# Cached GQA block on one core: x loaded in six pieces, five V loads made whole

## The chip, the core and the metric

The kernel runs on one core of a Trainium2 chip. The metric is the device time of one execution in microseconds (us). The core has a matmul engine (PE), a vector engine (DVE), a scalar engine (ACT), GpSimd (POOL) and a sync engine (SP); SP, and once ACT, issue the DMA transfers between device memory and the on-chip buffers. Sixteen DMA engines carry them.

## What is computed

One attention block of a decoder with a KV cache: 8 sequences of 4 new tokens, 32 query heads on 8 KV heads, 2048 cached positions, head size 128, all in bf16.

```python
B, Sq, D = 8, 4, 512
Hq, Hkv, Sk, Dh = 32, 8, 2048, 128
q = (x @ wq).reshape(B, Sq, Hq, Dh).transpose(0, 2, 1, 3)
k = jnp.repeat(k_cache, Hq // Hkv, axis=1)
v = jnp.repeat(v_cache, Hq // Hkv, axis=1)
scores = jnp.einsum("bhqd,bhkd->bhqk", q, k) * (Dh ** -0.5)
p = softmax(scores, axis=-1)
o = jnp.einsum("bhqk,bhkd->bhqd", p, v)
return o.transpose(0, 2, 1, 3).reshape(B, Sq, Hq * Dh) @ wo
```

x is 32 rows of 512 (32 KB). The K cache and the V cache have 33.6 MB each, wq and wo 4.2 MB each.

## The kernel before

The work is cut into eight units, u = 0 to 7. A unit is 16 pairs of a sequence and a KV head handled in two "members", 4 MB of K and 4 MB of V. Units 1 to 6 take one sequence each (`single(u)`); units 0 and 7 take half of the heads of the last two sequences. For a unit, DVE transposes K in 32 by 32 blocks (`turn`, L213), PE multiplies it with the queries (`scores`, L251), DVE takes the maxima (`top`), ACT the exponentials (`exps`, L291), DVE and the others bring the weights into place (`weights`, L305 and L315), and PE multiplies them with V (`values`, L331). `values` works on the unit before, so that two units overlap. Each matmul of `values` reads both members of V at one key position.

The order of the work on every engine is the program's order (`manual_schedule`); the framework adds the semaphores and the waits.

The big loads share a **ring** of four slots of 4 MB (`ring`, `NR = 4`). `loads` lists them in order: K0 (with x), wq, K1, V0, K2, V1, K3, V2, ... K7, V6, V7, wo. `issue(done)` takes the next of them as long as fewer than `done + 4` have been taken; a load into a slot waits until the slot's earlier content has landed and been read. `issue(0)` at the start issues K0, x, wq, K1 and V0; the call at the end of each unit's turn issues the next two.

`load_kv` can issue a load as one DMA (`whole`), as two halves of every row (`by_half`), or as one DMA for each member (`by_member`, 2 MB each). K0 goes by member, one on SP and one on ACT; V0 to V4 and K7 are in the list `split` and go by member on SP; V7 goes by half; wo goes in five pieces (L146). x is loaded on SP behind SP's half of K0 (L163), and is first used by four PE transposes (L416), whose result feeds the query projection with wq (L425). The projection's result is turned (L436) and copied into `q_bd` (L231), from where the scores of unit 0 take it.

At the end `project` (L403) multiplies the rows with wo; the last piece of wo is followed by a few matmuls, two copies out of PSUM (L482, L483) and the store of the result (L484).

Of the kernel before, what the change touches and what calls it, by code (L numbers as in the profile page):

```python
# [17 lines left out]
def kernel(  # L18
# [9 lines left out]
    nc = tc.nc  # L28
# [6 lines left out]
    T = B * Sq  # L35
# [6 lines left out]
    NU = B * Hkv // (G * NB)  # L42
# [31 lines left out]
    x_sb = const.tile([T, D], BF16, name="x_sb")  # L74
# [35 lines left out]
    def load_kv(kind, u, parts, engines=(nc.sync,)):  # L110

        slot = take((kind, u))
        cache = k_cache if kind == "k" else v_cache
        n = C * Dh
        if not single(u):
            rows = cache[NS1:, G * half_of(u) : G * half_of(u) + G].rearrange(
                "b g (s c) d -> (g s) b (c d)", c=C
            )
        elif kind == "v":
            rows = cache[u - 1].rearrange("(b g) (s c) d -> (g s) b (c d)", g=G, c=C)  # L120
        else:
            rows = cache[u - 1].rearrange("h (s c) d -> (h s) (c d)", c=NS * C)
        if kind == "k" and single(u):
            pairs = [(ring[:, slot, :, :].rearrange("p b n -> p (b n)"), rows)]
        elif parts is by_member:
            pairs = [(ring[:, slot, b, :], rows[:, b]) for b in range(NB)]
        else:
            pairs = [
                (ring[:, slot, :, int(h0 * n) : int(h1 * n)], rows[:, :, int(h0 * n) : int(h1 * n)])
                for h0, h1 in parts  # L130
            ]
        for i, (to, of) in enumerate(pairs):
            engines[i % len(engines)].dma_start(to, of)

    def load_wq():
        slot = take("wq")
        nc.sync.dma_start(
            ring[:, slot, :, :].rearrange("p b n -> p (b n)"), wq.rearrange("(p r) n -> p (r n)", r=R)
        )

    def load_wo():
        slot = take("wo")
        for gg, cuts in ((0, (0, RW)), (1, (0, 8, 13, 15, RW))):
            rows = wo[gg * G * 512 : (gg + 1) * G * 512, :].rearrange("(p r) j -> p (r j)", r=RW)
            for r0, r1 in zip(cuts, cuts[1:]):
                nc.sync.dma_start(ring[:, slot, gg, r0 * D : r1 * D], rows[:, r0 * D : r1 * D])  # L146
# [5 lines left out]
            loads.append(("k", u + 2))  # L152
    loads.append("wo")
    loads.reverse()
    split = [("v", 0), ("v", 1), ("v", 2), ("v", 3), ("v", 4), ("k", NU - 1)]

    def issue(done):

        while loads and n_loads[0] < done + NR:
            what = loads.pop()  # L160
            if what == "k0":
                load_kv("k", 0, by_member, (nc.sync, nc.scalar))
                nc.sync.dma_start(x_sb[:, :], x.flatten_outer_dims())  # L163
            elif what == "wq":
                load_wq()
            elif what == "wo":
                load_wo()
            elif what in split:
                load_kv(*what, by_member)
            else:  # L170
                load_kv(*what, by_half if what == ("v", NU - 1) else whole)

    issue(0)

    make_identity(nc, ident[:])
# [266 lines left out]
    for u in range(NU + 1):  # L442
# [19 lines left out]
        if u >= 1:  # L462
# [7 lines left out]
            if u == NU:  # L470
                joined(u - 1)
        issue(2 + 2 * u)

    o_last = psum_o.tile([128, DH], FP32, tag="o", name="o_last")
# [40 lines left out]
```

## Time and profile before

| | |
|---|---|
| Time, median of 3 runs | 184.73 us (184.65 to 189.89) |
| Profiled execution | 184.38 us, span from first to last instruction 182.5 us |
| Busy: PE, DVE, ACT, POOL | 136.6, 128.7, 70.3, 39.3 us |
| Read from device memory | 75.53 MB, 414 GB/s over the span |
| DMA transfers: K 10, V 14, wq 1, wo 5, x 1, result 1 | most of 2 or 4 MB |

The span counts from the first instruction to the last; the time of the execution includes 1.9 us around it. "Busy" of an engine is the time in which it had an instruction at work. The strip of the DMA line has 40 slices of 4.6 us; a 9 is 90% or more. For a DMA the profile gives the moment of issue on its queue (SPq, ACTq) and the time from issue until it has landed.

### The profile page before, as it was taken

The numbers are of one execution on the slowest core, as the hardware profiler recorded it, in microseconds if no ns is written. First come the engines' busy times: TensorE is split into PE (matmuls) and PEld (weight loads), VectorE is DVE, ScalarE is ACT, GpSimd is POOL, SyncE is SP. The second block draws the span as 40 slices with busy tenths as digits, with TensorE's granted clock in tenths as the row PEclk, the third lists the DMA queues.
The fourth block names the chain that finished last, engine by engine and source line by source line (L and its number), as shares of the span: only waits on it lengthen the run. The fifth ranks groups of instructions, "written<-read, shape, count | busy, mean of one in ns | idle before, by whom it ended". The sixth has DMA issues, their size and how long they took to land.

```text
span 182.5 us, 2386 instructions
## 1 busy us (share of the span) xinstructions
PE 136.6 (75%) x924; PEld 83.3 (46%) x924; DVE 128.7 (71%) x161; ACT 70.3 (39%) x91; POOL 39.3 (22%) x110
## 2 busy tenths in 40 slices
PE   0000076940999999998999898989399977899993
PEld 0000022310348635843783485358234852388971
DVE  6518025738994999599689957995399559967340
ACT  2000020019604940990395079109900792063010
POOL 8800006006200700430080035004400220023000
PEclk9999999995589999999999999999969999999999
DMA  6999999999999998999999999999999999999991
GB/s 226 431 485 395 424 460 406 424 445 449 452 384 427 456 461 382 420 460 452 391 417 453 460 402 418 431 478 424 391 435 424 435 427 435 415 426 438 427 385 42
DMA packets 4938, 75.70 MB, mean 415 GB/s; under 512 B 512, under 2 KB 704, under 8 KB 960
## 3 DMA queue, kind: packets, MB, share of 16 engines
q1 hardware_dynamic: 4784, 73.47, 94.3%
q10 hardware_dynamic: 144, 2.10, 2.8%
q8 instruction: 7, 0.11, 0.2%
q14 instruction: 3, 0.02, 0.0%
HBM read 75.53 MB, written 0.03 MB: 414 GB/s over the span
## 4 chain that ended last, share of the span: by engine, by line
DMA 42%; DVE 23%; PE 22%; issue 4%; ACT 3%; POOL 2%; SPq 1%; ACTq 0%; DVEq 0%; POOLq 0%
DMA ring<-in_wo_dram 16%; PE s_ps L251 16%; DMA ring<-in_k_cache_dram 15%; DVE kt L213 14%; DMA ring<-in_wq_dram 12%; DVE stat L264 4%; PE o_ps L331 4%; ACT p_sb L291 3%; PE psq L425 2%; DVE pt L305 2%; DVE stat L322 1%; POOL p_bd L315 1%; POOL q_bd L231 1%; PE s_ps L403 1%; DVE stat L272 0%
## 5 line engine op out<-in xcount | busy, mean ns | idle before, releaser
L251 PE MATMUL s_ps<-kt,q_bd 128*128 128x512 bf16 x256 | 69.5, 409 | 20.0 <-POOL q_bd L231 9.9
L213 DVE STREAM_TRANSPOSE kt<-ring 128x1024 f32<-128x1024 f32 x64 | 73.9, 1210 | 14.2 <-DMA ring<-in_k_cache_dram 11.4
L331 PE MATMUL o_ps<-ring,p_bd 128*128 128x256 bf16 x512 | 57.2, 273 | 0.0
L251 PEld LDWEIGHTS <-q_bd 128*128 128x128 bf16 x256 | 25.3, 102 | 63.0 <-issue 26.6
L331 PEld LDWEIGHTS <-p_bd 128*128 128x128 bf16 x512 | 49.8, 98 | 6.0 <-issue 0.2
L315 ACT COPY p_bd<-pt 32x1024 bf16<-32x1024 bf16 x44 | 45.8, 1041 | 1.5 <-DVE pt L305 1.1
L291 ACT ACTIVATE p_sb<-s_ps,stat 128x1024 bf16<-128x1024 f32 x16 | 17.7, 1110 | 72.2 <-DVE stat L272 72.2
L315 POOL COPY p_bd<-pt 32x1024 bf16<-32x1024 bf16 x16 | 17.0, 1065 | 105.9 <-DVE pt L305 93.2
L264 DVE TENSOR_REDUCE stat<-s_ps 128x1 f32<-128x1024 f32 x16 | 19.3, 1208 | 3.4 <-PE s_ps L251 3.4
L305 DVE STREAM_TRANSPOSE pt<-p_sb 128x512 f32<-128x512 f32 x16 | 11.4, 712 | 14.0 <-ACT p_sb L291 14.0
L231 POOL COPY q_bd<-qT 32x64 bf16<-32x64 bf16 x64 | 13.1, 231 | 20.7 <-DVE qT L436 19.0
L425 PE MATMUL psq<-ring,xT_sb 128*32 128x512 bf16 x32 | 3.6, 630 | 9.1 <-DMA ring<-in_wq_dram 9.1
L416 PE MATMUL xtp<-ident,x_sb 32*128 32x32 bf16 x4 | 0.3, 195 | 13.3 <-DMA x_sb<-in_x_dram 13.3
L436 DVE STREAM_TRANSPOSE qT<-q_sb 128x64 f32<-128x64 f32 x8 | 1.2, 214 | 8.8 <-ACT q_sb L432 8.8
L177 DVE MEMSET p_bd<- 128x2048 uint32 x3 | 5.3, 1765 | 2.0 <-PEq L499 1.2
L322 DVE TENSOR_SCALAR stat<-of_b,stat 128x2 f32<-128x2 f32 x8 | 6.3, 793 | 0.3
L416 PEld LDWEIGHTS <-x_sb 32*128 32x128 bf16 x4 | 0.2, 117 | 13.3 <-DMA x_sb<-in_x_dram 13.3
L425 PEld LDWEIGHTS <-xT_sb 128*32 128x32 bf16 x32 | 1.3, 140 | 10.5 <-issue 10.1
L432 ACT CAST q_sb<-psq 128x512 bf16<-128x512 f32 x2 | 1.2, 586 | 11.8 <-PE psq L425 11.8
L375 PEld LDWEIGHTS <-perm 128*128 128x128 bf16 x56 | 3.8, 97 | 2.0 <-issue 0.5
L419 ACT COPY xT_sb<-xtp 128x128 bf16<-128x128 bf16 x1 | 0.3, 266 | 11.2 <-PE xtp L416 11.2
L343 ACT ACTIVATE o_sb<-o_ps,stat 128x128 bf16<-128x128 f32 x8 | 2.9, 368 | 4.1 <-PE o_ps L331 3.9
(30 smaller groups left out, 46.4 us busy)
## 6 DMA issues: line engine op xcount, KB each, us to landing
ring<-in_k_cache_dram SPq DMA_DIRECT2D x6, 4096.0 KB, 22.7
ring<-in_v_cache_dram SPq DMA_DIRECT2D x12, 2048.0 KB, 23.6
ring<-in_v_cache_dram SPq DMA_DIRECT2D x2, 4096.0 KB, 29.6
ring<-in_k_cache_dram SPq DMA_DIRECT2D x3, 2048.0 KB, 27.2
ring<-in_wq_dram SPq DMA_DIRECT2D x1, 4096.0 KB, 21.0
ring<-in_k_cache_dram ACTq DMA_DIRECT2D x1, 2048.0 KB, 12.4
ring<-in_wo_dram SPq DMA_DIRECT2D x1, 2048.0 KB, 25.9
ring<-in_wo_dram SPq DMA_DIRECT2D x1, 1024.0 KB, 28.2
```

What stands on the lines that cost most here:

```text
L177: nc.vector.memset(t[:, :, :, :, :], 0.0)
L213: nc.vector.transpose(out=out, in_=in_)
L231: nc.gpsimd.tensor_copy(out=qb[k * 32 : (k + 1) * 32, m, :, g, b, :].rearrange("w (j e) q -> w j e q", e=2), in_=qT[of * 32 : (of + 1) * 3 ...
L251: nc.tensor.matmul(s_ps[t // 2][:, t % 2, :], lhsT=q_bd[u % 2][:, m, 2 * j + e, :, :, :].rearrange("w g b q -> w (g b q)"), rhs=rhs, start ...
L264: nc.vector.tensor_reduce(out=stats[u][0][:, h : h + 1], in_=s_ps[h][:, :, :].rearrange("q t n -> q (t n)"), axis=AX, op=ALU.max, negate=True,
L291: nc.scalar.activation(out=out, in_=in_, func=EXP, bias=stats[u][1][:, :], scale=scale, accum_out=stats[u][2][:, h : h + 1],)
L305: nc.vector.transpose(out=pt[:, :, :, :].rearrange("s c q e -> s (c q e)").bitcast(FP32), in_=ps[u, h][:, :, :, :].rearrange("q c s e -> q ...
L315: copy(out=pb[rows, :, g, :, :], in_=pt[rows, :, :, :])
L322: nc.vector.tensor_scalar_mul(stats[u][3][:, :], of_b[:, :], stats[u][4][:, :])
L331: nc.tensor.matmul(o_pss[u][:, :, :], lhsT=pbs[u, h][:, i // 2, :, :, i % 2].rearrange("s g q -> s (g q)"), rhs=v[:, :, key_of(u, h, i // ...
L375: nc.tensor.matmul(o_pms[r // 2][:, r % 2, gg, :], lhsT=perm[:, r, w : w + 128], rhs=o_sbs[u][:, b, :], start=(u == 0 and r % 2 == 0 and g ...
L425: nc.tensor.matmul(psq[g * T : (g + 1) * T, :], lhsT=xT_sb[:, r, :], rhs=w[:, (g * NB + gg) * rep * Dh : (g * NB + gg + 1) * rep * Dh], st ...
```

## The change

x is loaded by six DMAs of 16, 8, 4, 2, 1 and 1 rows instead of one of 32, at the same place, behind K0 and ahead of wq. V0 to V4 are no longer in `split`: each is one DMA of 4 MB instead of two of 2 MB. K7 stays split. The number of DMAs is the same as before, and no other line is changed.

```diff
-    split = [("v", 0), ("v", 1), ("v", 2), ("v", 3), ("v", 4), ("k", NU - 1)]
+    split = [("k", NU - 1)]
...
             if what == "k0":
                 load_kv("k", 0, by_member, (nc.sync, nc.scalar))
-                nc.sync.dma_start(x_sb[:, :], x.flatten_outer_dims())
+
+                cuts = (0, 16, 24, 28, 30, 31, T)
+                for t0, t1 in zip(cuts, cuts[1:]):
+                    nc.sync.dma_start(x_sb[t0:t1, :], x.flatten_outer_dims()[t0:t1])
```

## The prediction

> **What bounds the kernel now.** I read the page's strips and its chain first, then the DMA issues, then stretches of a microsecond at both ends, then SP's queue.
>
> ```profile
> DMA  6999999999999998999999999999999999999991
> GB/s 226 431 485 395 424 460 406 424 445 449 452 384 427 456 461 382 420 460 452 391 417 453 460 402 418 431 478 424 391 435 424 435 427 435 415 426 438 427 385 42
> ...
> HBM read 75.53 MB, written 0.03 MB: 414 GB/s over the span
> ...
> DMA 42%; DVE 23%; PE 22%; issue 4%; ACT 3%; POOL 2%; SPq 1%; ACTq 0%; DVEq 0%; POOLq 0%
> ```
>
> The DMA engines are full from the first slice to the last but one, while DVE (71%) and PE (75%) have room. The chain names DVE and PE for long stretches only because it goes back through SP's waits for a free ring slot; those waits end before the DMA queue is empty. At 35.01 us SP issues K2, and V0 is still in transfer until 2.68 + 36.7 = 39.4 us for the median of its two halves; at 53.43 it issues K3, with V1 in transfer until 62.4. The DMA engine never starves between 2 and 178 us, so whatever delays its stream moves the end by as much, and whatever else changes moves nothing.
>
> The start and the end of that stream, each row a stretch in us, then the busy time of the engines, the granted clock, the DMA share and GB/s:
>
> ```profile
> 0.00:1.00 1.00, 0.00 (x0) 0.00 (x0) 0.00 (x0) 0.00 (x0) 0.42 (x5) 1.00 0.00 0
> 1.00:2.00 1.00, 0.00 (x0) 0.00 (x0) 0.76 (x1) 0.83 (x1) 0.97 (x2) 1.00 0.69 197
> 2.00:3.00 1.00, 0.00 (x0) 0.00 (x0) 1.00 (x1) 0.45 (x1) 1.00 (x2) 1.00 0.88 279
> 3.00:4.00 1.00, 0.00 (x0) 0.00 (x0) 0.62 (x2) 0.00 (x0) 1.00 (x2) 1.00 0.84 328
> 4.00:12.00 8.00, 0.00 (x0) 0.00 (x0) 3.11 (x4) 0.00 (x0) 4.26 (x10) 1.00 1.01 433
> ...
> 12.00:13.00 1.00, 0.00 (x0) 0.00 (x0) 0.03 (x1) 0.00 (x0) 0.00 (x0) 1.00 1.17 488
> 13.00:14.00 1.00, 0.32 (x4) 0.21 (x4) 1.00 (x1) 0.27 (x1) 0.00 (x0) 1.00 1.21 524
> ```
>
> A packet is counted where it starts, so a share over 1 is a full stream. Between 12 and 14 us, where K0 ends and wq follows, there is no dip. That is the place to watch.
>
> SP's queue and the landings:
>
> ```profile
> 0.75 0.38 SPq L133 DMA_DIRECT2D ring<-in_k_cache_dram  x1
> 1.19 0.41 SPq L163 DMA_DIRECT2D x_sb<-in_x_dram  x1
> 1.65 0.41 SPq L137 DMA_DIRECT2D ring<-in_wq_dram  x1
> 2.11 0.53 SPq L133 DMA_DIRECT2D ring<-in_k_cache_dram  x1
> 2.68 1.02 SPq L133 DMA_DIRECT2D ring<-in_v_cache_dram  x2
> 35.01 0.33 SPq L133 DMA_DIRECT2D ring<-in_k_cache_dram  x1
> ```
> ```profile
> ring<-in_wq_dram SPq DMA_DIRECT2D x1, 4096.0 KB, 21.0
> ring<-in_k_cache_dram ACTq DMA_DIRECT2D x1, 2048.0 KB, 12.4
> ...
> x_sb<-in_x_dram SPq DMA_DIRECT2D x1, 32.0 KB, 12.1
> ```
>
> K0's ACT half is issued at 0.74 and lands 12.4 later, at 13.1; wq, issued at 1.65, has been waiting behind K0 in the queue for ten microseconds by then.
>
> **The semaphores.** The records of the DMA instructions name the semaphore that each raises. The 31 loads and the store share eight, strictly in turn: the two halves of K0 take the first two, x the third, wq the fourth, K1 the fifth, V0's halves the next two, K2 the eighth, and V1's halves start again with K0's two. Before SP reuses one it waits for the earlier load: ahead of K3, which takes x's semaphore, SP's record waits for x's as well, though K3 and x share no memory. Now all earlier loads have long landed when their turn comes round. After the change K0's two halves and six pieces of x take all eight, so **wq is the ninth** and must wait on SP until K0's half has landed. Behind wq on SP stand K1 and V0; PE waits for wq (L425), DVE later for K1. This wait is what I expect to decide the time.
>
> **The change part by part.**
>
> *Five more x issues on SP.* Five at 0.41 to 0.53 us (rows L163 and L133) are 2.1 to 2.7 us: SP reaches wq near 4.0 instead of 1.65. K0's transfer covers that until 12 us; without this cover it would cost about 2.3.
>
> *wq waits for K0.* In the trace of before SP's next wait for K0 (it stands ahead of K2) ends at 13.14. So wq is issued at 13.18. From an issue into an empty queue to the first packet the trace shows 1.01 us (K0 on SP: 0.75 to 1.76, with the sixteen engines starting from 1.76 to 2.08) and 1.10 (the store of the result, 180.17 to 181.27). wq's first packets then start between 14.19 and 14.51, mean 14.34. Before, the first packets of wq (32 KB each) start between 11.96 and 12.66, mean 12.31. The engines stand still for 14.34 - 12.31 = **2.03 us** on average.
>
> *The restart.* How slowly a drained queue picks up in mid-kernel isn't shown. Nearest is the start: 279 and 328 GB/s in two stretches that could carry 433 lose (154 + 105) / 433 = 0.6 us; summed over the packet records (16 KB packets of 0.61 us that took up to 1.37) it is 0.54 per engine. The bounds are 0 and 0.54. At the start two queues begin together, here one with packets twice as long, and HBM and queue have been at work: I take **0.3**, about the middle.
>
> *x's pieces on the DMA engines.* A 1 KB row takes 0.046 us and its semaphore write 0.009 in the records. If the pieces of 8, 4, 2 and 1 rows run on as many engines, one engine carries six rows and six writes, 0.33 us, where it carried two rows and one write, 0.10. These 0.23 us fall into the standstill: 0. Without it, up to 0.23 on one engine. The Trainium skill (DMA: Bandwidth & Descriptors, "Why a DMA increments its semaphore by 16 and not by 1") has a transfer run on the largest count up to 16 that divides its slowest dimension, and on the lowest-numbered engines, which is this uneven load; no run shown here has a transfer of fewer than 16 rows. By that rule alone the sum would be +0.2.
>
> *PE's transposes of x* wait for six semaphores instead of one; x lands at 13.3 to 13.5 and wq is due 11 us later: 0.
>
> *V0 to V4 whole.* The matmuls of L331 read both members at every step, so a split load released nobody earlier. Bytes and 16 KB packets stay; each split load took one semaphore write more per engine, 5 x 0.009 = **-0.05 us**. Five SP issues of 0.42 go, after waits of many microseconds, with a full queue: 0. V5 and V6 are whole already and flow at the same rate.
>
> *What comes after.* Every slot and every compute step moves with its load, so the margins of 4 us and more ahead of K2, 9 ahead of K3, stay. The last piece of wo lands at 151.39 + 28.0 = 179.4, the span ends at 182.5; these 3.1 us are unchanged.
>
> **Sum:** 2.03 + 0.3 - 0.05 = +2.3 us. The profiled execution took 184.38 (span 182.5), so 186.7 (span 184.8). The median of the runs, 184.73, lies 0.35 above that execution; for a median I say **187.0**. Bounds: the engine that was latest (12.66) restarting first and without loss is 14.19 - 12.66 = 1.5, less 0.4 if K0's half lands sooner with no wq packets between its own, 1.1 in all; the earliest engine (11.96) restarting last with full loss is 14.51 + 0.54 - 11.96 = 3.1, and 0.23 more if x's rows delay that half: 3.3. That is 185.8 to 188.0.
>
> **Rivals.** *No standstill* (not slower). It decides if SP can issue wq more than 1.0 us before K0's engines run dry at 12.0, so if the wait ends before 11 us or isn't made. Then x's uneven rows remain: -0.05 to +0.2, or a gain if they even the engines out: the sixteen landings of wo's last piece go from 177.5 to 179.4, mean 178.4, so at best -0.9. Time 183.8 to 184.9, most likely 184.7. For it: a queue 10 us deep. Against it: the wait at K3, and a count that comes to exactly eight ahead of wq.
>
> *A restart that costs much more* (slower by over 2%). At the start 433 GB/s is reached only after 4 us; if wq, K1 and V0, each issued 0.5 us after the other, each pick up with 0.54 of loss, the sum is 2.03 + 3 x 0.54 = 3.7, so 188.4 or above. For it: K0's two halves were both slow. Against it: packets run at 0.61 from 4 us on.
>
> *Small pieces in series.* If each piece of x had to finish before the next began, at the 1.5 us that the store of 32 KB takes from issue to landing, five more are 7.5 us: 184.73 + 7.5 = 192.2. Against it: the pieces of wo of 256 and 128 KB, on the same queue, land at 179.1 and 179.4, only 0.3 apart. The Trainium skill (DMA: Bandwidth & Descriptors, "Rules for kernel authors") says to join small transfers into one and calls those under 64 KB mostly overhead; with the fixed 2.0 us that its section "Anatomy of one DMA" gives, five would be an estimated 10 us in series. The landings of wo speak for overlap.
>
> **How the numbers follow.** The standstill has 0.85, no standstill 0.08, the dear restart 0.04, the series 0.03. The range is that of the standstill with a tenth more at each end, 185.7 to 188.1; it leaves out the other cases and a little of its own, no more than 2 in 10. A measurement here tells about 2% from no change: 181.0 and 188.4. No case reaches 181.0: faster 0.01. Slower by over 2% is the dear restart and the series, 0.07. The rest, 0.92, is within 2%, most of it over a per cent slower.
>
> **What would show it.** Right: SP waits 9 us for K0 at L137 ahead of wq; the DMA share between 13 and 14 us falls near 0; wq lands 11 to 12 us after its issue, near 25.0 instead of 22.7, and the first matmul of L425 with it; K2's issue, every later load and the last piece of wo come 2 to 2.6 us later; the tail stays 3.1. Wrong: wq issued by 4 us; no dip; a lag that grows after 25 us, or shrinks.

## The result, and the profile after

The changed kernel takes 187.38 us (median of 5 runs, 187.22 to 187.53) against 184.73 before: a ratio of 1.0148, 95% interval 1.0137 to 1.016, so 2.5 to 3.0 us slower. The forecast was 187.0, range 185.7 to 188.1. The profiled execution took 187.28 us, span 185.3, which is 2.8 to 2.9 more than the one of before. In some executions of several kernels, the one before included, a stretch of the DMA stream runs at fewer GB/s and the time is 3 us or more longer; every ratio here leaves these out, and both profiles of the kernel under "A wait that ends early" are of such executions.

The page of the changed kernel, strips and chain:

```profile
DMA  6959999999999999999899999999999999999991
GB/s 233 438 241 354 446 446 453 393 428 431 446 424 424 484 391 416 435 456 453 382 424 442 460 446 391 421 446 446 403 435 428 431 435 428 414 430 431 430 384 44
...
HBM read 75.53 MB, written 0.03 MB: 408 GB/s over the span
...
DMA 45%; DVE 26%; PE 17%; issue 5%; ACT 3%; POOL 2%; SPq 0%; ACTq 0%; DVEq 0%; POOLq 0%
```

The same bytes went at 408 GB/s instead of 414. What differs is one place: the third slice (9.3 to 13.9 us) has a 5 and 241 GB/s, and the fourth 354, where before there were a 9 and 485, and 395. From the fifth slice on, DMA is as full as before. The stretches of a microsecond around it (columns as in the prediction; the last two are DMA share and GB/s):

```profile
12.00:13.00 1.00, 0.00 (x0) 0.00 (x0) 0.00 (x0) 0.00 (x0) 0.00 (x0) 1.00 0.13 41
13.00:14.00 1.00, 0.28 (x4) 0.21 (x4) 0.97 (x1) 0.00 (x0) 0.00 (x0) 1.00 0.00 0
14.00:15.00 1.00, 0.00 (x0) 0.10 (x1) 1.00 (x2) 0.27 (x1) 0.00 (x0) 1.00 1.79 492
15.00:16.00 1.00, 0.00 (x0) 0.00 (x0) 1.00 (x2) 0.00 (x0) 0.00 (x0) 1.00 0.16 66
```

Not one packet starts between 13 and 14 us. Between 14 and 15 fifteen of the sixteen engines start their first packet of wq (492 GB/s in one us is 15 packets of 32 KB, counted whole where they start); between 15 and 16 only two packets start (66): the first ones are still on their way. In the packet records these first sixteen take 1.87 us on average, where a packet of 32 KB took 1.21 before.

SP's queue and its waits:

```profile
0.75 0.37 SPq L133 DMA_DIRECT2D ring<-in_k_cache_dram  x1
1.17 2.06 SPq L166 DMA_DIRECT2D x_sb<-in_x_dram  x6
13.18 0.36 SPq L137 DMA_DIRECT2D ring<-in_wq_dram  x1
13.58 0.43 SPq L133 DMA_DIRECT2D ring<-in_k_cache_dram  x1
14.06 0.43 SPq L133 DMA_DIRECT2D ring<-in_v_cache_dram  x1
37.43 0.33 SPq L133 DMA_DIRECT2D ring<-in_k_cache_dram  x1
```
```profile
SPq L137 <- DMA ring<-in_k_cache_dram: 9.9, 1, 9.9
```

wq is issued at 13.18 instead of 1.65, after a wait of 9.9 us for K0. Its record waits for the semaphore that K0's ACT half raises, and raises the same one. K2 is issued 2.4 us later than before. From wq's issue to its landing, and the first matmul on it, before and after:

```profile
ring<-in_wq_dram SPq DMA_DIRECT2D x1, 4096.0 KB, 12.2
```
```profile
22.72 3.61 PE L425 MATMUL psq<-ring,xT_sb 128*32 128x512 bf16 x32 [9.07 <-DMA ring<-in_wq_dram]
25.41 3.61 PE L428 MATMUL psq<-ring,xT_sb 128*32 128x512 bf16 x32 [11.43 <-DMA ring<-in_wq_dram]
```

wq lands at 13.18 + 12.2 = 25.4, 2.7 later than before; by the trace's semaphore records the last piece of wo lands at 182.17 instead of 179.35, 2.8 later, and the span ends 3.1 us behind it in both kernels. The large loads between them land 2.6 to 2.9 later by the same records. So the 2.7 us are lost between 12 and 16 us and carried to the end.

### The profile page after: what moved, and what is told of

The parts are those of the page before. It is cut to its first block, busy times and chain, and to the rows that moved or that the text cites. A ratio compares the mean times of both kernels' runs of the same rounds, so it can differ in the third digit from the quotient of the medians.

```text
span 185.3 us, 2388 instructions
## 1 busy us (share of the span) xinstructions
PE 135.1 (73%) x924; PEld 83.1 (45%) x924; DVE 128.6 (69%) x161; ACT 70.2 (38%) x91; POOL 39.3 (21%) x110
## 4 chain that ended last, share of the span: by engine, by line
DMA 45%; DVE 26%; PE 17%; issue 5%; ACT 3%; POOL 2%; SPq 0%; ACTq 0%; DVEq 0%; POOLq 0%
DMA ring<-in_k_cache_dram 22%; DVE kt L216 18%; DMA ring<-in_wo_dram 16%; PE s_ps L254 10%; DMA ring<-in_wq_dram 7%; DVE stat L267 4%; PE o_ps L334 4%; ACT p_sb L294 3%; PE psq L428 2%; DVE pt L308 2%; DVE stat L325 1%; POOL p_bd L318 1%; POOL q_bd L234 1%; PE s_ps L406 1%; DVE stat L275 0%
## 5 line engine op out<-in xcount | busy, mean ns | idle before, releaser
L254 PE MATMUL s_ps<-kt,q_bd 128*128 128x512 bf16 x256 | 68.0, 402 | 21.5 <-POOL q_bd L234 9.9
L406 PE MATMUL s_ps<-ring,oP 128*32 128x256 bf16 x32 | 4.2, 272 | 0.5 <-DMA ring<-in_wo_dram 0.5
## 6 DMA issues: line engine op xcount, KB each, us to landing
ring<-in_wq_dram SPq DMA_DIRECT2D x1, 4096.0 KB, 12.2
```

The costliest lines, as they stand in the source:

```text
L254: nc.tensor.matmul(s_ps[t // 2][:, t % 2, :], lhsT=q_bd[u % 2][:, m, 2 * j + e, :, :, :].rearrange("w g b q -> w (g b q)"), rhs=rhs, start ...
L406: nc.tensor.matmul(out_ps[half], lhsT=oP[gg][:, r, :], rhs=w[:, r, half * DH : (half + 1) * DH], start=(gg == 0 and r == 0), stop=(gg == N ...
```

## The experiments

The theory: x's six pieces and K0's two halves use up the eight DMA semaphores, wq waits for K0's landing, and the DMA engines run dry and restart. Rivals: the pieces themselves cost (by number, or by loading the DMA engines unevenly); the whole V loads cost; any wait of SP costs.

### One part of the change at a time

x in pieces, V by member as before:

```diff
-    split = [("k", NU - 1)]
+    split = [("v", 0), ("v", 1), ("v", 2), ("v", 3), ("v", 4), ("k", NU - 1)]
```

> x in six pieces, V0 to V4 by member as before. Theory (wq is the ninth DMA, waits for K0's half and lets the DMA engines run dry): all of the loss, about 2.7 us more than before, 187.4. Rival (whole V loads cost): none of it, 184.7. DMA share between 13 and 14 us: near 0 by the theory, over 1 by the rival.

Measured: ratio 1.0161 (1.0130 to 1.0191), wq issued at 13.30, 0 GB/s between 13 and 14 us. The whole loss is here.

V whole, x in one piece: the other half of the diff alone.

> V0 to V4 whole, x in one piece. Theory: wq is the fourth DMA and waits for nothing; five semaphore writes fewer, so 184.7 or up to 0.1 less. Rival (whole V loads cost): 187.4.

Measured: ratio 1.0007 (0.9993 to 1.0020), wq issued at 1.64. V's part neither costs nor brings anything that can be measured; the 0.05 us of its semaphore writes are smaller than the interval can show.

### One semaphore fewer

```diff
-                cuts = (0, 16, 24, 28, 30, 31, T)
+                cuts = (0, 16, 24, 28, 30, T)
```

> As the changed kernel, but the last two single rows of x go together: pieces of 16, 8, 4, 2 and 2. Theory: K0's two halves and five pieces leave the eighth semaphore to wq, which waits for nothing; K1 is now the ninth and waits until 13 us, with wq in transfer until 22: no dip, 184.7 (184.5 to 184.9). Rival (each small piece of x costs its share of the 2.65 us, 0.53 for each of the five added): 184.7 + 4 x 0.53 = 186.8. Rival (the uneven load of the DMA engines costs): about 187.2, since the first engine still carries five rows of the former six.

Measured: ratio 0.9998 (0.9986 to 1.0010). SP's queue and the stretches around 13 us of this kernel:

```profile
1.17 1.74 SPq L166 DMA_DIRECT2D x_sb<-in_x_dram  x5
2.95 0.36 SPq L137 DMA_DIRECT2D ring<-in_wq_dram  x1
13.57 0.35 SPq L133 DMA_DIRECT2D ring<-in_k_cache_dram  x1
```
```profile
12.00:13.00 1.00, 0.00 (x0) 0.00 (x0) 0.00 (x0) 0.00 (x0) 0.00 (x0) 1.00 1.29 539
13.00:14.00 1.00, 0.14 (x4) 0.17 (x4) 0.60 (x1) 0.00 (x0) 0.00 (x0) 1.00 1.23 524
```

To join two single rows takes the whole loss away. wq is issued at 2.95 and stands in the queue when K0 ends; the same wait now falls on K1, at 13.57, with wq still in transfer, and costs nothing. Number and unevenness of the pieces are refuted as causes of the 2.7 us: five of six are still there, and the one engine that all of them would use has five rows of the former six. The interval leaves room for about 0.2 us either way.

### Six even pieces

```diff
-                cuts = (0, 16, 24, 28, 30, 31, T)
+                cuts = (0, 96, 192, 288, 352, 416, D)
                 for t0, t1 in zip(cuts, cuts[1:]):
-                    nc.sync.dma_start(x_sb[t0:t1, :], x.flatten_outer_dims()[t0:t1])
+                    nc.sync.dma_start(x_sb[:, t0:t1], x.flatten_outer_dims()[:, t0:t1])
```

> x in six pieces of all 32 rows, cut by columns (96, 96, 96, 64, 64, 96), so that all sixteen DMA engines carry the same. Theory: wq is the ninth again, so the whole loss, 187.2 to 187.6. Rival (uneven load of the engines): 184.7.

Measured: ratio 1.0149 (1.0130 to 1.0169), wq issued at 13.50, 1 GB/s between 13 and 14 us. Evenly loaded engines lose the same.

### The six pieces behind wq

The `for` of the pieces moves from the branch of K0 to the branch of wq, behind `load_wq()`.

> x's six pieces stand behind wq instead of ahead of it. Theory: wq is the third DMA and waits for nothing; x's last piece and K1 wait for K0 until 13, with wq in transfer until 22.5: no dip. x lands behind wq, so the queries of unit 0 come about 1 us later, off the stream's path (K2 is issued at 36 with V0 in transfer until 42): 184.7 to 184.9. Rival (the six pieces themselves cost): 187.4. If the start of the compute decides instead of the DMA stream: 185.7.

Run a second time, for an interval:

> The same kernel as in wq_first, for an interval: six pieces of x behind wq. Theory: ratio 0.999 to 1.002, although the first matmul of the projection starts 1.3 us later than before. Rival (the six pieces cost): 1.014.

Measured: ratio 0.9998 (0.9976 to 1.0021). SP and the first matmuls of that run:

```profile
1.18 0.42 SPq L137 DMA_DIRECT2D ring<-in_wq_dram  x1
1.65 11.82 SPq L167 DMA_DIRECT2D x_sb<-in_x_dram  x6
13.52 0.36 SPq L133 DMA_DIRECT2D ring<-in_k_cache_dram  x1
```
```profile
23.93 3.60 PE L427 MATMUL psq<-ring,xT_sb 128*32 128x512 bf16 x32 [0.35 <-ACT xT_sb L421]
```

All six pieces are there, SP waits for K0 until 13.5 (now at the last piece), and the projection starts 1.2 us later than before (22.72), and none of it shows in the time: a later start of the compute is not on the path, the DMA stream is.

### A wait that ends early

K0 goes in four DMAs, half a member each, and x in four pieces, so that wq is the ninth DMA still:

```diff
...
+        elif parts is by_quarter:
+            pairs = [
+                (ring[:, slot, b, i * n // 2 : (i + 1) * n // 2], rows[:, b, i * n // 2 : (i + 1) * n // 2])
+                for i in range(2)
+                for b in range(NB)
+            ]
...
-                load_kv("k", 0, by_member, (nc.sync, nc.scalar))
+                load_kv("k", 0, by_quarter, (nc.sync, nc.scalar))
-                cuts = (0, 16, 24, 28, 30, 31, T)
+                cuts = (0, 16, 24, 28, T)
```

> K0 in four DMAs of 1 MB (half a member each, on SP and ACT in turn) and x in four pieces (16, 8, 4, 4): wq is the ninth again, but the load whose semaphore it takes is now a first quarter of K0, which lands near 7 us. Theory: SP waits until about 7, wq is in the queue well before K0 ends at 12, no dip: 184.7 to 185.0. If any wait of wq costs, whenever it ends: by 3.5 us more than an issue at 1.65 as against 9 to 10, a third of the loss or more, 185.6 and up.

This one too was run a second time:

> The same kernel as in quarters, for a profile without a disturbance and for an interval: K0 in four DMAs, x in four pieces, wq is the ninth DMA and its wait ends at 8.2 us, before K0 ends. Theory: no dip at 13 us, last piece of wo near 179.4, ratio 0.998 to 1.002. If a wait of wq costs whenever it ends: ratio 1.005 or more.

Measured: ratio 0.9999 (0.9977 to 1.0022). wq is issued at 8.34, after a wait of 5.2 us for the first quarter, and the stream has 590 and 492 GB/s in the stretches from 12 and 13 us:

```profile
8.34 0.36 SPq L144 DMA_DIRECT2D ring<-in_wq_dram  x1
```
```profile
12.00:13.00 1.00, 0.00 (x0) 0.00 (x0) 0.81 (x1) 0.00 (x0) 0.00 (x0) 1.00 1.44 590
13.00:14.00 1.00, 0.19 (x4) 0.21 (x4) 0.00 (x0) 0.00 (x0) 0.00 (x0) 1.00 1.27 492
```

K0's last packet ends at 12.7 by the packet records. A wait on a reused semaphore that ends 4 us before the queue runs out is free here.

### x ahead of SP's half of K0

The pieces are issued before `load_kv("k", 0, ...)`.

> x's six pieces ahead of SP's half of K0. wq is the ninth and waits for the ACT half of K0, as in the changed kernel. SP's half of K0 is issued 2 us later, so the ACT half has the engines alone for about 2 us and lands near 10 to 11 instead of 13.1, while the other half keeps the engines at work until 12.3. Theory: wq is issued 1 to 2 us before they run dry, so nearly all of the loss is gone: 184.6 to 185.3, by how much of the 1.0 us from issue to first packet is covered. Rival (pieces, their number or unevenness, or the wait itself): 187.4.

Measured: ratio 1.0107 (1.0065 to 1.0149), runs from 185.6 to 187.3. The theory's number is missed, and so is the rival's. The profiled run took 186.08; two of the other three took 187.2 and 187.3, as long as the changed kernel, and there is no trace of those. SP in the profiled run, and the stretches from 12 us:

```profile
0.75 1.97 SPq L164 DMA_DIRECT2D x_sb<-in_x_dram  x6
2.75 0.36 SPq L133 DMA_DIRECT2D ring<-in_k_cache_dram  x1
11.85 0.35 SPq L137 DMA_DIRECT2D ring<-in_wq_dram  x1
```
```profile
12.00:13.00 1.00, 0.00 (x0) 0.00 (x0) 0.00 (x0) 0.00 (x0) 0.00 (x0) 1.00 1.26 442
13.00:14.00 1.00, 0.00 (x0) 0.00 (x0) 0.00 (x0) 0.00 (x0) 0.00 (x0) 1.00 1.36 459
```

K0's ACT half landed at 11.8, not at 10 to 11, so wq's packets came at 12.85, just as the engines ran out: no standstill is left, but wq's first packets still took 1.61 us on average (1.21 to 2.10) instead of 1.21. By the packet records three things lengthen packets: the start loses 0.85 us per engine instead of 0.54; K0's 16 KB packets take 0.71 us instead of 0.61 from 8.6 us on, about 0.6 in all; wq's first packets lose 0.4. That is 0.3 + 0.6 + 0.4 = 1.3 of the 1.6 by which the span is longer. Why the packets ran at 0.71 is open, and so is what the two longer runs lost. The trace shows that the standstill goes when the wait ends sooner, and that this order has costs of its own.

### How the restart is paid

```diff
-        nc.sync.dma_start(
-            ring[:, slot, :, :].rearrange("p b n -> p (b n)"), wq.rearrange("(p r) n -> p (r n)", r=R)
-        )
+        rows = wq.rearrange("(p r) n -> p (r n)", r=R)
+        for i in range(NB):
+            nc.sync.dma_start(ring[:, slot, i, :], rows[:, i * C * Dh : (i + 1) * C * Dh])
```

> The changed kernel with wq in two DMAs of 2 MB (rows of 16 KB instead of 32). The standstill stays. It is on how the restart is paid, 0.65 us per engine in the changed kernel, all in the first packet of each engine (1.87 us instead of 1.21 for 32 KB). If the restart is a stretch of about 1.9 us at two thirds of the rate: the first two 16 KB packets are slow, again 0.6 in all, 187.4. If it is the first packet's length that grows by half whatever its size: 0.3, so 187.0 to 187.1.

Measured: ratio 1.0147 (1.0130 to 1.0164), 187.24 us; the intervals do not part the two forms, the packets do. The stretches of this kernel:

```profile
13.00:14.00 1.00, 0.10 (x4) 0.13 (x4) 1.00 (x1) 0.00 (x0) 0.00 (x0) 1.00 0.00 0
14.00:15.00 1.00, 0.18 (x4) 0.17 (x4) 1.00 (x2) 0.27 (x1) 0.00 (x0) 1.00 1.16 262
15.00:16.00 1.00, 0.00 (x0) 0.00 (x0) 1.00 (x2) 0.00 (x0) 0.00 (x0) 1.00 0.76 311
```

The first 16 KB packets of wq take 1.16 us on average instead of 0.61, and nearly all of the second ones are at full speed again. With 32 KB it is 1.87 instead of 1.21. The loss sits almost wholly in the first packets, 0.55 us on average with 16 KB and 0.66 with 32 KB, and hardly depends on their size. Neither form that was put up had that: it is not half of the packet's time (that would be 0.3), and not spread over two packets. The two rows of 262 and 311 GB/s look like a slow rate over two microseconds; the second packets, at full speed, say otherwise.

It is not the same delay for every engine either. In the changed kernel the thirteen first packets that start within 0.4 us of the earliest lose 0.73 us on average, and the one that starts 1.0 us after it loses 0.07. With the even pieces eleven lose 0.80, and the five that start 0.7 to 0.9 us late lose 0.2 or less; with x alone in pieces fourteen lose 0.65, and the two that start 0.6 and 0.9 us late lose 0.38 and 0.23. That looks like a slow first microsecond of the whole stream rather than a price that each engine pays. No run was made to part the two, and the cause stays open.

No run beats the kernel before; the nearest, with ratios of 0.9998 to 1.0007, are the same.

## Why the prediction was right

*What bounds the kernel.* Right: the loss is made at 12 to 16 us, and the 2.69 us at wq's landing are 2.82 at wo's. The six pieces behind wq delay the first matmul by 1.2 us and cost nothing. One sign was put wrongly: not every load is issued 2 to 2.6 us later. SP issues the loads from V2 to V5 only 1.1 us later than before (V2 at 63.53 instead of 62.45), and they land 2.6 to 2.9 later all the same. The stream carries the lag, whatever the moments of issue; why these come closer is open.

*The wait of wq for its semaphore.* Right, and shown from both sides: present in all kernels that lose 2.5 to 3 us, gone with one piece fewer, harmless where it ends at 8.3 us.

*The standstill.* Put at 2.03 us; the first packets of wq now start at 14.16 to 15.16, mean 14.40, against a mean of 12.28 before, so 2.12. (The 12.31 of the prediction is the middle between the earliest and the latest, not the mean. Its second case for the time from issue to first packet is misread too: the first packet of the result's store starts at 181.02, 0.85 us after the issue, and 181.27 is where its last one starts. The sum rests on K0's 1.01, which wq repeated.) Three engines started after the 14.51 that the start of the kernel had suggested, the last at 15.16.

*The restart.* This term was mis-sized: 0.3 taken between bounds of 0 and 0.54, measured 1.87 - 1.21 = 0.66, outside the upper bound. The reason for the middle value, that queue and memory had been at work, did not hold: a drained stream lost at least as much in mid-kernel as at the start. With it the sum is 2.12 + 0.66 - 0.05 = 2.7 instead of 2.3, and 184.73 + 2.7 = 187.4 is what was measured.

*x's five more issues.* Put at 2.1 to 2.7 us; all six take 2.06, the five added 1.65, since a piece of four rows or fewer takes 0.25 to 0.29 us on SP. Hidden, as said.

*x's pieces on the engines.* Nothing that can be measured, as said: 0.9998 with five pieces, where the 0.2 us that the prediction allows without a standstill would not stand out. The pieces of 8, 4, 2, 1 and 1 rows have 8, 4, 2, 1 and 1 semaphore records when they land near 13 us, the load of all 32 rows had 16; each has one record more at 2.1 to 3.4 us, just behind its issue. The Trainium skill (DMA: Bandwidth & Descriptors, "Why a DMA increments its semaphore by 16 and not by 1") has each engine in use raise the semaphore once at landing, and the sequencer write the rest at once; the counts in this trace agree.

*The rivals.* The dear restart was right that the restart costs more and wrong on repetition: wq pays once, K1 and V0 not at all. The series of small pieces is out: x's last row lands at 13.57, 0.24 behind its first sixteen rows. The 2.0 us in the estimate of 10 us stand in the Trainium skill (DMA: Bandwidth & Descriptors, "Anatomy of one DMA") for DMAs issued from GpSimd, and SP issues x's pieces. The Trainium skill (DMA: Bandwidth & Descriptors, "Rules for kernel authors") calls transfers under 64 KB mostly overhead; queued behind a large one, pieces of 1 to 16 KB cost no time here, except by the semaphore that each takes.

*V whole.* Nothing that can be measured: 1.0007. The -0.05 us of the sum is too small for any run here to show.

## What to carry to other kernels

Count the DMAs in flight ahead of a load that keeps the stream full: here the ninth waits for the first, whatever its size, and a 1 KB load counts as much as a 4 MB one. Look at what is queued when such a wait ends, since wq's first packet came 1.0 us after its issue. With 4 us of transfers still queued the wait was free. With about 1.0 us (x ahead of K0) there was no standstill, but the first packets still lost 0.4 us. With nothing queued the standstill and a restart of 0.66 us were lost, and stayed lost to the end of this DMA-bound kernel. Stretches of one microsecond show such a hole plainly, where the mean of the whole span, 408 GB/s instead of 414, hides it.

## What the runs showed that was not expected

A drained DMA stream restarts slowly: the first packets of the sixteen engines took 0.55 us (16 KB) and 0.66 us (32 KB) longer on average, on top of 1.0 us from issue to first packet. Engines that started 0.6 us or more behind the earliest lost between nothing and 0.38 us. SP issues a small DMA faster: 0.25 to 0.29 us for four rows or fewer, 0.36 for eight, 0.42 for sixteen.
